# The fifth unit's second matmul: half by seven block products, with the weight sums made earlier

## The chip, the cores and the metric

The kernel runs on one core of a Trainium2 chip. The metric is the device time of one execution in microseconds (us). The kernel before takes 2752.74 us, the median of three runs between 2751.86 and 2753.47. One further execution was recorded by the profiler; every duration below comes from it.

The engines are named as in the profile: PE (matrix products), DVE (vector), ACT (activation and copies), POOL (a second vector engine) and SP, whose queue issues all the data transfers (DMAs) in the order of the program.

## The reference

Two kinds of layer alternate, twice each, on a sequence of 2048 tokens with 1024 channels:

```python
x = A_q
x = x + _A_ref(_layernorm(x), A_k, A_v, A_shift_k, A_ssm_k, A_ssm_D)
x = x + _B_ref(_layernorm(x), B_w1, B_b1, B_w2, B_b2)
x = x + _A_ref(_layernorm(x), A_k, A_v, A_shift_k, A_ssm_k, A_ssm_D)
x = x + _B_ref(_layernorm(x), B_w1, B_b1, B_w2, B_b2)
```

`_A_ref(q, k, v, ...)` takes a causal convolution along the sequence of four taps on `k`, multiplies by `v`, applies a second causal convolution that is as long as the sequence (one filter for each channel), and multiplies by `q`. Only `q` is the layer's input; the convolved signal depends on `k`, `v` and the filters alone, so it is the same in both layers and is computed once. `_B_ref` is the dense part: `h = x @ w1 + b1` (1024 to 3584), `h = relu(h)**2`, `out = h @ w2 + b2` (3584 to 1024). All data is float32.

## The kernel before, in words

**Units.** The sequence is cut into four blocks of 512 tokens. A unit is one layer pair on one block: first the gate with the convolution and two normalisations, then the two dense matmuls. The eight units run in the order `ORDER` (line 25), as (layer, block): (0,0), (1,0), (0,1), (0,2), (1,1), (0,3), (1,2), (1,3). They are numbered from 0, so the fifth unit is unit 4, layer 1 on block 1.

**Precision.** Each float32 operand is split into a rounded high part and the rest, and each product is made of three matmuls: high by high, high by low, low by high (`mm3`, line 326).

**Steps.** The dense part of a unit is a list of steps, written by `add` (line 867). A first-matmul step `m1` uses half of one of the 28 weight tiles of `w1` and makes 12 matmuls of 128x128 by 128x512. A second-matmul step `m2` uses one half-width tile of `w2` and makes 12 as well, three for each of four groups of 128 tokens. A plain unit has four chunks of seven tiles: 56 `m1` and 56 `m2` steps, 112 in all. Within a chunk the first `m2` half is followed by the two `m1` steps of the next chunk's first tile.

**The block products.** In units 5, 6 and 7 (`WINO`, line 51) the second matmul is done in 2x2 blocks with seven products in place of eight (`add_wino`, line 873). Two neighbouring tiles of `h` form a pair, so there are 14 pairs, in four groups of 3, 3, 4 and 4 (`WCH`). A step `w2` handles one product of one pair and makes six matmuls; a pair needs seven of them where plain work needs four `m2` steps of 12. Such a unit has 56 `m1` steps and 98 `w2` steps. Three of the seven products take blocks of `w2` as they are; four take sums of weight blocks. `relu_w` (line 1454) makes the sums of the `h` blocks on DVE (four subtractions or additions and the low parts) and ACT. The results stay in seven accumulators (`wacc`, `load_wacc`, line 1490); `evict_w` adds each finished product to them, by ACT copies the first time where the accumulator is empty; `merge_w` combines them at the end, and `store_w` writes them out. The bias is added to four of them by `add_b2w` on POOL.

**The weight sums.** `make_t` (line 1410) makes the sums of weight blocks once. It works in 28 parts (14 pairs by two column halves): two loads of 256 KB from `w2`, four DVE subtractions of 128x256, two stores of 256 KB into the DRAM tiles `td`. It is a generator: the main loop resumes it once per step, or by a fraction `T_RATE` of a step (lines 1803 to 1809), and it begins when the convolution is done. Its tiles are free buffers of the convolution. A weight load that needs a sum not yet made resumes the generator until it is there (`w_load`, line 973).

**The weight pipeline.** For each step a weight tile is loaded eight steps ahead, its high part is made by ACT (line 997) four ahead and its low part by DVE (line 1005) three ahead. Many split tiles are kept in DRAM after their first use (`wd_m`, `wd_t`); such a pair of 512 KB is read back into one of six `whl` buffers, four steps ahead (line 995), and needs neither ACT nor DVE. In chunk 1 of a unit every tile is such a pair, in other chunks about half.

**What runs beside it.** The long convolution (`prod_stream`, line 511) works through blocks 1 to 3 while the units run. Its products are POOL multiplications (line 517) followed by DVE reductions (line 521); a finished group goes through PE (`inverse`) and is stored in `yd` (line 574). `pace[u]` (line 1666) sets how much of it each step issues: the convolution's whole work for a block divided by the number of steps available less `PACE_SLACK`. `close_conv` (line 1676) issues what is left when the next unit needs it. A block counts as done only in a step's own tick after its last store.

**The next unit's input.** `prep_a` (line 724) reads the next unit's `x` from the 28th step on, in four 512 KB tiles of a ring of two (`px`), and takes statistics. After a plain unit `prep_b` does the gate, the second normalisation and the transposes in the last 18 steps. In units 5 and 6 `prep_w` (line 803) does the first half for each token group early (`W_EARLY`, counted in steps before the end), stores it, and the rest from step 30 before the end on. `load_b2` (line 1638) takes a tile of the same `px` ring for the bias: 12 steps into a plain unit, 34 steps into a unit of block products (line 1693).

**Order.** The engines execute what a step issues in program order. A ring buffer that is asked for again makes the asking instruction wait for the last use of its old content, even if that use is issued in a later step.

Of the kernel before, what the change touches and what calls it, by code (L numbers as in the profile page):

```python
# [46 lines left out]
PACE_SLACK = {1: 74, 3: 10}  # L47
# [187 lines left out]
def tile_h3_mlp(ctx: ExitStack, tc: tile.TileContext, q, kT, vT, shk, ssmT, ssmD, w1, b1, w2, b2,  # L235
# [567 lines left out]
    def prep_w(l, b, lag):  # L803
# [49 lines left out]
        for tt in range(NT):  # L853
            for k, d in enumerate((0, 4, 5, 7)):
                lag.at(W_PREP - W_EARLY[tt] + d, early, tt, k)
            for k, d in enumerate((0, 5, 7, 8, 9)):
                lag.at(W_PREP - W_LATE + 5 * tt + d, late, tt, k)
# [15 lines left out]
    def add_wino(u):  # L873
        p0 = 0
        for c, n in enumerate(WCH):
            pairs = range(p0, p0 + n)
            p0 += n
            for f in range(2 * pairs[0], 2 * pairs[-1] + 2):
                for kh in range(2):
                    add("m1", u, f // FC, f % FC, kh)  # L880
            for j in WORD_END if c == len(WCH) - 1 else WORD:
                for p in pairs:
                    f = 2 * p + (j > 0)
                    wsrc.append(("m2", f // FC, int(j == 2), f % FC) if j < 3 else ("t", p, (j - 4) % 4, 0))
                    if c < len(WCH) - 1:
                        single.add(len(wsrc) - 1)
# [523 lines left out]
    def make_t():  # L1410
        parts = [(p, dq) for p in range(FT // 2) for dq in range(2)]
        got = {}

        def places(n):
            if n < T_FIRST:
                nm, m = (("cp", 3), ("cx", 2), ("cg", 2))[n % 3]
                t = cv.tile([P, 2, 2, 256], F32, name=nm, bufs=m)
                return [t[:, 0], t[:, 1]]
            return [pool.tile([P, 2, 256], F32, name=nm, bufs=m) for pool, nm, m in (
                [(cv, "sm", 2)] * 2, [(const, "fh", 1), (const, "fl", 1)], [(ml, "yt", 2)] * 2)[n % 3]]  # L1420

        def load(n):
            if n < len(parts):
                p, dq = parts[n]
                got[n] = places(n)
# [5 lines left out]
        load(0)  # L1431
        yield
        load(1)
        yield
        yield
        for n, (p, dq) in enumerate(parts):
# [6 lines left out]
            yield  # L1443
            load(n + 2)
            yield
            if n >= T_FIRST:
                yield
# [432 lines left out]
```

## Time and profile before

| | |
|---|---|
| runs | 2752.74 us median (2751.86 to 2753.47) |
| the profiled execution | 2754.0 us, its span 2752.2 us |
| PE busy | 2696.8 us, 98% of the span, 12632 matmuls |
| PE weight loads | 2238.5 us, beside the matmuls |
| DVE busy | 2010.1 us, 73% |
| ACT busy | 1121.7 us, 41% |
| POOL busy | 922.5 us, 34%, nearly all before 1730 us |
| granted PE clock | 0.9955 on average |
| DMA | 755.9 MB, 275 GB/s on average |

The span is the time from the first to the last recorded instruction. A matmul's recorded duration (about 390 ns) overlaps the next one's; the distance between two starts says what one costs. In rows of the timeline the first number is the start, the second the duration. The window rows give the window, its length, the busy time of PE, PE's weight loads, DVE, ACT and POOL with the number of instructions, then the granted PE clock, the busy share of the DMA engines and GB/s. In the rows of waits the numbers are the total wait, the number of waits and the longest, all in us.

### The profile page before, as it was taken

What the parts mean: (1) busy time and instruction counts of PE and PEld (TensorE: products, weight loads), DVE (VectorE), ACT (ScalarE), POOL (GpSimd) and SP (SyncE); (2) the same over time, 40 slices, a digit from 0 to 9 for tenths busy, and PEclk for the clock granted to TensorE, in tenths of its full rate; (3) what the DMA queues carried; (4) which work ended last, traced back from release to release, by engine and by line L of the source; (5) the groups of instructions that cost most, each with busy time, mean ns of one, the idle gap of its engine ahead of it and who ended that gap; (6) DMA issues with size and microseconds to landing.
All of it is one profiled execution on the core that took longest, in us unless ns stands there. A gap on an engine that the chain in (4) does not pass through costs nothing.

```text
span 2752.2 us, 36801 instructions
## 1 busy us (share of the span) xinstructions
PE 2696.8 (98%) x12632; PEld 2238.5 (81%) x12632; DVE 2010.1 (73%) x3109; ACT 1121.7 (41%) x1935; POOL 922.5 (34%) x655
## 2 busy tenths in 40 slices
PE   7899999899999999999999999999999999999999
PEld 6888787788888888888888888888788788878887
DVE  8879888779888877788777665366687666664555
ACT  4254344343444333342234422254455444445443
POOL 6926665155542655326544454000100010001000
PEclk9999999999999999999999999999999999999999
DMA  8489988689989898788987877688888866676546
GB/s 261 164 295 334 306 294 288 238 281 376 345 290 316 306 335 298 257 318 294 344 280 250 314 277 266 226 290 304 297 289 294 281 228 210 230 258 208 176 165 203
DMA packets 378876, 755.86 MB, mean 275 GB/s; under 512 B 43704, under 2 KB 160576, under 8 KB 378688
## 3 DMA queue, kind: packets, MB, share of 16 engines
q1 hardware_dynamic: 378688, 753.50, 79.7%
q8 instruction: 100, 1.64, 0.2%
q14 instruction: 88, 0.72, 0.1%
HBM read 603.41 MB, written 149.95 MB: 274 GB/s over the span
## 4 chain that ended last, share of the span: by engine, by line
PE 84%; DVE 6%; DMA 5%; POOL 2%; issue 1%; ACT 1%; SPq 1%; DVEq 0%; ACTq 0%; POOLq 0%
PE p L327 26%; PE p L329 26%; PE p L328 26%; DMA whl<-wd_m 1%; DMA wr<-w 1%; PE pt L329 1%; PE pt L328 1%; PE pt L327 1%; DVE whl L1005 1%; DMA cg<-gd 1%; DMA whl<-wd_t 1%; PE p L1076 1%; PE pt L446 0%; PE pt L412 0%; PE pt L588 0%
## 5 line engine op out<-in xcount | busy, mean ns | idle before, releaser
L517 POOL TENSOR_TENSOR cp<-cx,cg 128x384 f32<-128x384 f32 (+5 forms) x288 | 540.9, 1891 | 587.7 <-DVE sm L521 383.6
L327 PE MATMUL p<-xh,whl 128*128 128x512 f32 (+1 forms) x1840 | 707.7, 385 | 2.0 <-DMA whl<-wd_m 1.9
L329 PE MATMUL p<-xh,whl 128*128 128x512 f32 (+1 forms) x1840 | 703.8, 382 | 0.6 <-POOL whl L1005 0.6
L328 PE MATMUL p<-xl,whl 128*128 128x512 f32 (+1 forms) x1840 | 703.6, 382 | 0.3 <-DVE xl L1323 0.3
L997 ACT CAST whl<-wr 128x512 fp32r<-128x512 f32 x638 | 384.4, 618 | 458.1 <-PE p L329 269.6
L1005 DVE TENSOR_TENSOR whl<-wr,whl 128x512 fp32r<-128x512 f32 x624 | 506.1, 831 | 72.9 <-ACT whl L997 66.9
L327 PE MATMUL p<-whl,rh 128*128 128x512 f32 x1372 | 547.4, 399 | 6.1 <-DMA whl<-wd_m 4.5
L328 PE MATMUL p<-whl,rh 128*128 128x512 f32 x1372 | 542.4, 395 | 4.2 <-DVE whl L1005 4.2
L329 PE MATMUL p<-whl,rl 128*128 128x512 f32 x1372 | 541.8, 395 | 0.0
L327 PEld LDWEIGHTS p<-xh,whl 128*128 128x128 f32 x1840 | 346.4, 188 | 71.0 <-DMA whl<-wd_m 2.0
L329 PEld LDWEIGHTS p<-xh,whl 128*128 128x128 f32 x1840 | 346.2, 188 | 68.9 <-POOL whl L1005 0.8
L328 PEld LDWEIGHTS p<-xl,whl 128*128 128x128 f32 x1840 | 346.2, 188 | 66.4 <-DVE xl L1323 0.5
L327 PEld LDWEIGHTS p<-whl,rh 128*128 128x128 f32 x1372 | 258.8, 189 | 67.3 <-DMA whl<-wd_m 7.7
L328 PEld LDWEIGHTS p<-whl,rh 128*128 128x128 f32 x1372 | 258.9, 189 | 63.7 <-DVE whl L1005 6.4
L329 PEld LDWEIGHTS p<-whl,rl 128*128 128x128 f32 x1372 | 258.7, 189 | 60.3
L1504 POOL TENSOR_TENSOR acc<-acc,px 128x512 f32<-128x512 f32 x18 | 23.1, 1323 | 774.7 <-DMA px<-b 774.7
L1407 DVE TENSOR_TENSOR rl<-wr,rh 128x512 fp32r<-128x512 f32 x140 | 142.2, 1016 | 179.9 <-ACT rh L1402 179.8
L521 DVE TENSOR_REDUCE sm<-cp 128x128 f32<-128x384 f32 (+5 forms) x288 | 249.0, 873 | 7.9 <-POOL cp L517 7.9
L1399 ACT ACTIVATE wr<-p,b1t 128x512 f32<-128x512 f32 x138 | 95.2, 690 | 371.6 <-PE p L329 369.8
L1468 DVE TENSOR_TENSOR rl<-wr,rh 128x256 fp32r<-128x256 f32 x84 | 49.4, 588 | 206.4 <-ACT rh L1463 206.3
L1527 DVE TENSOR_TENSOR acc<-p,acc 128x512 f32<-128x512 f32 x152 | 101.2, 687 | 89.2 <-PE p L329 88.6
L1460 ACT ACTIVATE wr<-p,b1t 128x512 f32<-128x512 f32 x84 | 57.9, 689 | 187.5 <-PE p L329 187.5
(270 smaller groups left out, 3437.1 us busy)
## 6 DMA issues: line engine op xcount, KB each, us to landing
whl<-wd_m SPq DMA_DIRECT2D x382, 512.0 KB, 5.6
wr<-w SPq DMA_DIRECT2D x494, 256.0 KB, 5.2
wr<-td SPq DMA_DIRECT2D x152, 256.0 KB, 4.4
wd_m<-whl SPq DMA_DIRECT2D x70, 512.0 KB, 6.5
cx<-xd SPq DMA_DIRECT2D x48, 512.0 KB, 5.4
cg<-gd SPq DMA_DIRECT2D x48, 512.0 KB, 6.9
gd<-fg SPq DMA_DIRECT2D x72, 256.0 KB, 6.2
cx<-xd SPq DMA_DIRECT2D x48, 384.0 KB, 6.0
```

The source lines that it names most:

```text
L327: PE.matmul(o, lh, rh, start=start, stop=False)
L328: PE.matmul(o, lh, rl, start=False, stop=False)
L329: PE.matmul(o, ll, rh, start=False, stop=stop)
L517: G.tensor_mul(pr.rearrange("p c i -> p i c"), xt[:, 0:j + 1], gt[:, j::-1])
L521: V.tensor_reduce(sm[:, ty, jj], st["pr"], axis=AX.X, op=OP.add)
L997: A.copy(t[:, 0], raws[n]["t"])
L1005: ENG[e[n % len(e)]].tensor_sub(t[:, 1], raws[n]["t"], t[:, 0].bitcast(F32))
L1399: A.activation(r, st["o"], AF.Relu, bias=b1t[:, st["f"]:st["f"] + 1])
L1407: V.tensor_sub(st["lo"], st["r"]["t"], st["hi"].bitcast(F32))
L1460: A.activation(r, st["o"], AF.Relu, bias=b1t[:, st["f"]:st["f"] + 1])
L1468: V.tensor_sub(st["lo"], r[:, 0:n], st["hi"].bitcast(F32))
L1527: V.tensor_add(accs[tt][:, d], o, accs[tt][:, d])
```

## The change

1. **Unit 4 joins.** `WINO` becomes a table of groups for each unit. Units 5, 6 and 7 keep theirs (written as first pair and count). Unit 4 gets two groups, pairs 7 to 9 and 10 to 13. Its chunks 0 and 1 stay plain (`m1` and `m2` steps), its tiles 14 to 27 go by block products. The unit has 28 `m2` and 49 `w2` steps beside its 56 `m1` steps, 133 in all. The plain chunks' results are added to the accumulators by a new `evict_c`.
2. **The unit's frame.** It thereby takes over what comes with block products: `load_wacc` at step 11 in place of `load_acc` at 5, the bias at steps 34 and 38 in place of 12 and 16, merges and stores of the accumulators into the next unit's first steps, and `prep_w` in place of `prep_b` for unit 5. The early parts of `prep_w` come 76, 69, 45 and 38 steps before the end; units 5 and 6 keep 87, 80, 45, 38.
3. **The weight sums begin with unit 4.** `make_t` takes pairs 7 to 13 first and then 0 to 6. While the convolution is unfinished it works on one part at a time, in the two `yt` buffers, one part in seven steps. Afterwards it works with two loads ahead, in three sets of buffers, one part in five resumptions. It is resumed once per step, in `w2` steps at a rate of 0.85 (unit 4's first group), 0.35 (its second) and 0.7 (later units).
4. **The convolution ends sooner.** `PACE_SLACK` for block 3 goes from 10 to 44 steps. `close_conv` is called 77 steps before the end of unit 4, that is at its step 55.
5. **Kept sums.** Split weight sums are kept in DRAM from unit 5 on, as before; unit 4's are not kept.

The core of the diff:

```diff
-PACE_SLACK = {1: 74, 3: 10}
+PACE_SLACK = {1: 74, 3: 44}
-WINO = (5, 6, 7)
+WINO = {4: ((7, 3), (10, 4)), **{u: ((0, 3), (3, 3), (6, 4), (10, 4)) for u in (5, 6, 7)}}
-W_PREP, W_EARLY, W_LATE = 90, (87, 80, 45, 38), 30
-T_KEPT, T_RATE, T_FIRST, T_AT = 10, 0.6, 10, (0, 3, 1, 2)
-WCH = (3, 3, 4, 4)
+W_EARLY, W_LATE = {4: (76, 69, 45, 38), 5: (87, 80, 45, 38), 6: (87, 80, 45, 38)}, 30
+T_KEPT, T_RATE, T_AT = 10, (0.35, 0.85, 0.7), (0, 3, 1, 2)
...
     def add_wino(u):
+        p0 = WINO[u][0][0]
+        for c in range(2 * p0 // FC):
+            for f in range(FC):
+                if f or c == 0:
+                    for kh in range(2):
+                        add("m1", u, c, f, kh)
+            for dh in range(2):
+                for i in range(FC):
+                    add("m2", u, c, dh, i)
+                if dh == 0:
+                    for kh in range(2):
+                        add("m1", u, c + 1, 0, kh)
+        for c, (first, n) in enumerate(WINO[u]):
+            pairs = range(first, first + n)
+            for f in range(2 * first, 2 * (first + n)):
+                if f == 0 or f > 2 * p0:
+                    for kh in range(2):
+                        add("m1", u, f // FC, f % FC, kh)
...
     def late_kept(key):
...
+        if k == "t":
+            return 5
...
-        if u or not late_kept(wsrc[w]):
+        if u >= late_kept(wsrc[w]):
...
+        n = 0
+        while NB - 1 not in done:
+            load(n, 0)
+            yield
+            yield
+            yield
+            yield from sums(n)
+            yield
+            yield
+            store(n)
+            n += 1
+            yield
+        first = n
+        load(n, 0)
+        yield
+        load(n + 1, 1)
+        yield
+        yield
+        while n < len(parts):
+            yield from sums(n)
+            yield
+            load(n + 2, (n + 2 - first) % 3)
+            yield
+            yield
+            store(n)
+            n += 1
+            yield
...
+    def evict_c(os, wacc, dh):
+        for tt, o in os.items():
+            a = wacc[(1, 2, 3, "x")[2 * (tt // 2) + dh]][tt % 2]
+            V.tensor_add(a, o, a)
...
-            if u in WINO and left == W_PREP:
-                nxt = prep_w(*ORDER[u + 1], lag)
+            if u in WINO and left == W_EARLY[u][0] + 1:
+                close_conv(ORDER[u + 1][1])
+                nxt = prep_w(*ORDER[u + 1], lag, W_EARLY[u])
...
-        if u >= WMAKE and len(done) == NB and not tgen:
+        if u >= WMAKE and not tgen:
             tgen.append(make_t())
         if tgen:
-            town += T_RATE if k == "w2" or u not in WINO and left <= 18 else 1
+            town += 1 if k != "w2" else T_RATE[2 if u > WMAKE else left >= 28]
```

More of the change, by code (lines that the diff above doesn't have):

```diff
@@ L873, in add_wino @@
     def add_wino(u):
[L874 to L881, printed above, removed]
+        p0 = WINO[u][0][0]
[16 more added lines that the diff above has]
+                        add("m1", u, f // FC, f % FC, kh)
+            last = c == len(WINO[u]) - 1
+            for j in WORD_END if last else WORD:
                 for p in pairs:
@@ L1429, in load, with sums @@
                     SY.dma_start(t, src[:, :, dq * 256:(dq + 1) * 256])
[L1431 to L1436, printed above, removed]
+        def sums(n):
             (b00, b01), (b10, b11) = (tuple(t[:, h] for h in range(2)) for t in got[n])
@@ L1442, in make_t, with store @@
             V.tensor_sub(b10, b10, b11)
[L1443 to L1447, printed above, removed]
+        def store(n):
+            p, dq = parts[n]
             for e, t in enumerate(got.pop(n)):
```

32 lines of the change are left out of this document (15 added, 17 removed).

## The prediction

> **What bounds the kernel now.** The page comes first: busy times and the chain that ended last.
>
> ```profile
> span 2752.2 us, 36801 instructions
> PE 2696.8 (98%) x12632; PEld 2238.5 (81%) x12632; DVE 2010.1 (73%) x3109; ACT 1121.7 (41%) x1935; POOL 922.5 (34%) x655
> PE 84%; DVE 6%; DMA 5%; POOL 2%; issue 1%; ACT 1%; SPq 1%; DVEq 0%; ACTq 0%; POOLq 0%
> ```
>
> PE is busy 98% of the span, and the chain lies on it. DVE, at 73%, is next. Next the windows: unit 4 whole, unit 5 whole, parts of unit 5, and one dense stretch of unit 1.
>
> ```profile
> 1543.00:1863.00 320.00, 320.00 (x1436) 263.45 (x1435) 182.88 (x274) 100.96 (x172) 102.65 (x59) 1.00 0.79 277
> 1863.00:2160.00 297.00, 294.06 (x1290) 238.64 (x1290) 223.61 (x429) 145.78 (x241) 10.66 (x8) 1.00 0.87 301
> 1893.20:1922.60 29.40, 29.40 (x128) 23.73 (x127) 21.65 (x40) 17.44 (x30) 0.00 (x0) 1.00 0.78 257
> 1922.60:1960.00 37.40, 35.83 (x156) 28.67 (x155) 22.96 (x49) 15.65 (x26) 10.66 (x8) 1.00 0.89 317
> 2040.00:2100.00 60.00, 60.00 (x263) 48.85 (x262) 48.75 (x96) 24.10 (x41) 0.00 (x0) 1.00 0.89 305
> 2100.00:2160.00 60.00, 58.63 (x269) 47.26 (x268) 48.89 (x85) 33.76 (x57) 0.00 (x0) 1.00 0.85 300
> 619.00:688.00 69.00, 69.00 (x321) 57.38 (x320) 65.27 (x83) 26.80 (x47) 41.52 (x28) 1.00 1.03 375
> ```
>
> PE never idles in unit 4; in unit 5 it idles 2.9 us, 1.6 in 1922.6 to 1960 and 1.4 at the end. In 619 to 688 DVE is 95% busy and the DMA engines are full, yet PE idles nowhere: load on both is not yet a cost. So fewer matmuls in unit 4 shorten the kernel, unless something arrives late. What a matmul costs stands in PE's timeline.
>
> ```profile
> 1542.86 0.39 PE L327 MATMUL p<-xh,whl 128*128 128x512 f32 x1
> 1628.29 0.40 PE L327 MATMUL p<-xh,whl 128*128 128x512 f32 x1
> 1860.55 0.39 PE L327 MATMUL p<-xh,whl 128*128 128x512 f32 x1
> 1893.21 0.40 PE L327 MATMUL p<-whl,rh 128*128 128x512 f32 x1
> 1905.76 0.39 PE L327 MATMUL p<-whl,cx 128*128 128x512 f32 x1
> 1922.56 0.39 PE L327 MATMUL p<-xh,whl 128*128 128x512 f32 x1
> 1942.92 0.50 PE L327 MATMUL p<-xh,whl 128*128 128x512 f32 x1 [1.13 <-DMA whl<-wd_m]
> 2158.26 0.47 PE L327 MATMUL p<-xh,whl 128*128 128x512 f32 x1 [0.31 <-DMA whl<-wd_m]
> 2453.33 0.50 PE L327 MATMUL p<-whl,rh 128*128 128x512 f32 x1 [1.81 <-DMA whl<-wd_m]
> 2455.34 0.77 PE L327 MATMUL p<-xh,whl 128*128 128x512 f32 x1
> 2455.90 0.63 PE L328 MATMUL p<-xl,whl 128*128 128x512 f32 x1
> ```
>
> From 1893.21 to 1905.76 lie 54 block-product matmuls on unsummed blocks of h, 0.2324 us each; from there to 1922.56 lie 72 on summed blocks, 0.2333 each. Unit 4 runs from 1542.86 to 1860.55, 317.7 us; unit 5 to 2158.26, 297.7.
>
> **The change part by part.**
>
> *Fewer matmuls.* 28 `m2` steps of 12 go (336), 49 `w2` steps of 6 come (294): 42 fewer. At 0.2324 us that is 9.8 us, all on PE's path. Of the 294, four products in seven (168) use summed blocks, 0.0009 us dearer: 0.2 back. For a matmul of 512 columns the Trainium skill ("TensorE: Matmul & The Clock Gate", Back-to-back issue gap) gives 512/2.4 + 2.5, about 216 ns, for the isolated spacing; by that the gain would be an estimated 9.1 us. The trace shows 232, and I keep it.
>
> *Weights, evictions, h sums.* By the code's counts, 14 of the 28 old weights came from kept pairs; of the 49 new ones 5 do and 44 are split: 30 more splits on DVE and ACT, 30 more loads of 256 KB and 9 fewer pair reads of 512 KB on SP (0.32 to 0.43 us an issue in the rows below). Per pair of tiles DVE also makes four sums and a long low part, and there are 20 more accumulator additions and merges. None of these is on PE. Their cover is unit 5: its first `w2` stretch has the same 21 split weights and keeps DVE 21.65 of 29.4 us busy with PE never idle. Unit 4's first stretch adds 0.25 resumption of the sums per step, 5 in all or one part (1.7 us below), and loses one of two statistics: about 24 of 29.4, 81%, as in 2040 to 2100, where PE doesn't idle. I take 0.3 us; ends 0 and 3.
>
> *The unit's end.* Merges, stores and the next unit's first loads crowd the queues there. Unit 5 loses 1.4 us so. Unit 6 loses 1.81 before 2453.33, and afterwards PE's starts are 0.56 us apart (2455.34, 2455.90), so a long gap costs more than itself. Unit 4's end has no `wd_t` transfers and is nearest to unit 5's. I take 1.4; ends 0 and 3.5.
>
> *The bias load at step 34.* This is the wait that the change adds.
>
> ```profile
> SPq L715 <- POOL fk L1504: 8.8, 1, 8.8
> 1937.91 0.32 SPq L715 DMA_DIRECT2D px<-x  x1
> 1938.34 0.37 SPq L995 DMA_DIRECT2D whl<-wd_m  x1
> 1643.36 0.33 SPq L715 DMA_DIRECT2D px<-q  x1
> 1649.31 1.27 DVE L686 BATCH_NORM_STATS2 st<-px 128x6 f32<-128x512 f32 x2
> DMA to landing us min/median/max: 3.2/4.2/6.6
> ```
>
> In unit 5 the last `px` load waits 8.8 us until POOL has added the bias that holds its buffer; SP's queue stands, the pair behind it is issued at 1938.34, and PE loses the 1.13 us above (1.6 with its followers). In unit 4 the bias load falls into `prep_a`. Two `px` tiles are in use, so SP stops at step 33 (the pair for step 36 is out by then) until the second statistics, which end at 1643.36 in the trace of before. Step 30 starts at 1628.29 and an `m1` step is 2.72 us, so that is step 35.5. The pair behind it, for step 37, lands a median 4.2 us (the pairs of 1600 to 1740) later, at 37.1: just late. Then the last `px` load waits for the third statistics (1650.6, step 38.2), and the pair for step 40 lands at 39.8. So I take unit 5's 1.6 us; ends 0 and 4 (both pairs at the 6.6 us landing, with followers). POOL's bias additions move from step 16 to 37, still beside the convolution; three product buffers cover them, the convolution's loads that stand behind the bias load on SP are issued two product groups ahead, and chunk 1's weights are pairs that need no DVE.
>
> *The convolution's pace.* Block 3's work is 92.2 in the code's units. Before it goes at 92.2/(2 x 96.8 - 10) = 0.502 a step, after at 92.2/(96.8 + 117.8 - 44) = 0.540 (96.8 and 117.8 are the steps, the last 19 of a unit counted by a fifth).
>
> ```profile
> 1730.76 0.52 SPq L574 DMA_DIRECT2D yd<-wr  x1
> 1725.98 0.75 DVE L554 TENSOR_TENSOR yl<-sm,yh 128x256 fp32r<-128x256 f32 x2
> 1738.29 0.42 DVE L1438 TENSOR_TENSOR cp<-cp 128x256 f32<-128x256 f32 x1
> ```
>
> Its last store is at 1730.76, about step 67.5 of unit 4. The (96.8 + 67.5) x 0.502 = 82.5 done in units 3 and 4 then take 152.7 steps, so it ends at step 55.9, twelve sooner. `close_conv` at step 55 therefore finds it finished: a block counts as done only in a step's tick, which the drain doesn't give. The early store lets the new early loads through. Nothing waits for the convolution, so its end earns nothing; its cover in units 3 and 4 (7.6% more per step) is the dense row 619 to 688. I take 0.
>
> *The sums beside the convolution.* About 8 of 28 parts now run before step 55, when POOL is busy.
>
> ```profile
> L1005 DVE TENSOR_TENSOR whl<-wr,whl 128x512 fp32r<-128x512 f32 x15 | 18.2, 1214 | 6.0 <-ACT whl L997 5.8
> L1005 DVE TENSOR_TENSOR whl<-wr,whl 128x512 fp32r<-128x512 f32 x20 | 13.7, 687 | 10.5 <-ACT whl L997 7.1 <-DMA wr<-w 3.4
> L517 POOL TENSOR_TENSOR cp<-cx,cg 128x1024 f32<-128x1024 f32 x48 | 124.8, 2599 | 138.1 <-DVE sm L521 123.3 <-DMA cx<-xd 14.8
> 1542.90:1730.00 187.10, 187.10 (x842) 154.42 (x841) 110.60 (x122) 51.06 (x89) 102.65 (x59) 1.00 0.77 281
> SPq L1429 <- DMA td<-yt: 5.7, 3, 4.8
> DMA to landing us min/median/max: 5.0/6.1/8.3
> ```
>
> A split takes 1214 ns beside POOL's products (1543 to 1700) and 687 after them (1740 to 1860), 0.53 more. A sum takes 0.42 alone (1738.29), so 0.95 here; a part of four took 1.7 alone. 32 sums are 30 us in the 155 us to step 55 (55 steps of 2.72 or 2.79 and the transforms); the present 110.6 us packed into that time make 141, 91%, below the 95% of unit 1. Each part's load also waits for the last one's store in the one `yt` set: the longest such wait in unit 5 is 4.8 us. A pair is issued about five steps, 13.6 us, before its use; less a 6.1 us landing (619 to 688) 7.5 are left. I take 0. In unit 5 the sums taken away free DVE, but its losses are queue waits: 0, at best 1 us gained. Total sum work and its transfers are unchanged.
>
> Sum: -9.8 + 0.2 + 0.3 + 1.4 + 1.6 = -6.3 us. The profiled execution, 2754.0 us, would be 2747.7; it is 1.3 above the median of the runs, so I forecast 2746.4. The ends give -10.6 and +0.9, or 2742.1 and 2753.6, if all fall together.
>
> **The rivals.**
>
> *A, whole gain.* The waits at step 33 to 40 are absorbed (4.2 us landings leave 37.1 against 37) and unit 5 gains: -9.8 + 0.2 + 0.3 + 0.4, 2743.8. Against it: unit 5 lost 1.6 us by this very wait.
>
> *B, the gain is eaten.* Both queue waits at their upper ends: -9.8 + 0.2 + 0.3 + 3.5 + 4 = -1.8, 2750.9. For it: DMA share 0.83 to 1.0 lengthens landings, and a gap slows PE after it. Against: no unit shows both.
>
> *C, slower: SP starves chunk 1.* Steps 33 to 56 read 24 pairs, one a step; the stops for `px` and for the `yt` set (steps 35, 42, 49) come so close that the queue never regains its five steps, and each pair is 1.13 us late. It decides from 7 late pairs (against 7.9 without the `px` term); with 16 late, 2752.7 - 7.9 + 18.1 = 2762.9. Against it: 7.5 us of slack against stops of 4.8.
>
> *D, slower: DVE blocked by POOL.* If a DVE sum waits out a whole product, 2.6 us, 32 sums cost 32 x 3.0 = 96 us and 110.6 + 96 exceed 155 by 52; a third of it reaching PE through late low parts of h gives 2752.7 - 6.3 + 17 = 2763. The Trainium skill ("SBUF — State Buffer", Who interferes with whom) says just this: a DVE instruction with two SBUF inputs and a POOL instruction that reads SBUF exclude each other for the whole instruction. The 1214 against 687 agrees that they meet, but the mean extra is a fifth of a product.
>
> *E, the block products don't shorten.* If `w2` steps waited on weights, 42 matmuls fewer would be time spent idle: 2752.7. Unit 5's 20 us against unit 4 speak against it.
>
> **How the numbers follow.** Forecast 0.47, A 0.14, B 0.22, C 0.08, D 0.05, E 0.04. A change under 0.2% (5.5 us) can't be told from none. Faster by more than that, under 2747.2: A, and most of the forecast's own range (2744.5 to 2748.3), 0.60. Within: B, E and the forecast's rest, 0.27. Slower: C and D, 0.13. The range, 2742.5 to 2752, leaves out C, D, E and the edge of A.
>
> **What would show it.** Right: 42 matmuls fewer; unit 4 about 311.5 us long; a first sum near 1552; the last `yd` store near 1698; SP standing at the bias load near 1634 to 1643, PE idle by 0.5 to 2 us at steps 37 to 40; unit 4's `w2` spacing 0.233. Wrong: PE waiting for `whl` in steps 42 to 56 (C), DVE over 95% before step 55 with PE waiting for low parts (D), or PE idle within the `w2` groups (E).

## The result and the profile after

The kernel after takes 2763.13 us (median; 2756.91 to 2773.73), the kernel before, on the same chip and beside it, 2757.05 us (2751.86 to 2763.14). The ratio is 1.0023, with a 95% interval of 1.0013 to 1.0032: slower by some 6 us. The forecast was 2746.4, with a range up to 2752.0, so both the number and the sign were wrong.

The page of the kernel after, one execution of 2761.69 us: its span, the busy times, and the chain that ended last.

```profile
span 2759.9 us, 36945 instructions
PE 2691.7 (98%) x12590; PEld 2232.1 (81%) x12590; DVE 2067.3 (75%) x3190; ACT 1143.1 (41%) x1972; POOL 925.9 (34%) x659
PE 78%; DMA 8%; DVE 8%; POOL 3%; issue 2%; SPq 1%; ACT 1%; DVEq 0%; POOLq 0%; ACTq 0%
```

PE has the 42 matmuls fewer, 5 us less busy time, and a smaller share of the chain: 78% in place of 84%, with DMA up from 5 to 8 and DVE from 6 to 8. So PE waits more than it saves.

Where it waits is found from the first matmul of each unit. Units 0 to 2 are the same instructions in both kernels and still differ between executions by up to 9 us (unit 3 starts at 1208.1 in the profile of before, at 1212.8 in that of after, and at 1217.5 in a further one of before, b0 below), so I compare from unit 3 on.

| us | unit 3 | unit 4 | unit 5 | unit 6 | unit 7, to the end |
|---|---|---|---|---|---|
| before | 334.7 | 317.7 | 297.7 | 297.1 | 296.9 |
| before, second profile (b0) | 333.6 | 317.7 | 297.7 | 296.7 | 295.7 |
| after | 336.1 | 324.0 | 297.7 | 295.1 | 294.2 |

Unit 4, which should have become 6.2 us shorter, is 6.3 longer, and most of what follows is about it. Two smaller things go beside it. Unit 3 is 1.4 to 2.5 us longer (the section on e16 comes back to it). Units 6 and 7 together are 3.1 to 4.7 us shorter, with PE idle for 1.9 us in them where it idled 4.0; the prediction had no term for that, and no run isolates its cause.

Unit 4 falls into three stretches: I from its start to step 30, II from there over the rest of chunk 1 and its second matmul to step 58, III to the end of the unit. The windows of before and then of after, in this order (length, then busy PE, weight loads, DVE, ACT, POOL with counts, clock, DMA share, GB/s):

```profile
1542.86:1628.29 85.43, 85.43 (x385) 70.47 (x384) 55.77 (x52) 24.41 (x42) 58.25 (x32) 1.00 0.84 307
1628.29:1706.80 78.51, 78.51 (x349) 64.54 (x348) 41.69 (x54) 18.01 (x32) 38.50 (x22) 1.00 0.82 302
1706.80:1860.55 153.75, 153.75 (x693) 126.54 (x692) 83.17 (x165) 57.91 (x97) 5.89 (x5) 1.00 0.75 246
```

```profile
1548.95:1634.14 85.19, 84.23 (x373) 69.04 (x372) 58.88 (x69) 24.65 (x43) 48.79 (x26) 1.00 0.92 334
1634.14:1723.10 88.96, 82.69 (x362) 66.87 (x360) 50.80 (x71) 18.43 (x33) 42.79 (x30) 0.98 0.87 315
1723.10:1872.96 149.86, 144.27 (x639) 116.45 (x638) 124.75 (x247) 77.58 (x131) 0.00 (x0) 1.00 0.85 291
```

Before, PE is busy in every microsecond. After, it idles 1.0 us in I, 6.3 in II and 5.6 in III. The faster convolution also moves some twelve matmuls of its inverse from I into unit 3 (385 to 373 records in I) and as many from III into II. To count losses alone I use lengths without a stop: I 84.0 (the shortest, in eight of the kernels below), II 80.0 (the kernel e5 below, which is before with the faster convolution), III 152.3 (e5) less the 9.6 us of matmuls that the forecast took off, 142.7. A loss counted so holds both PE's idle time and the slow starts that can follow a stop. By that the kernel after loses 1.2 us in I, 9.0 in II and 7.2 in III, 17.4 in all; the forecast had 3.3 (0.3 + 1.4 + 1.6).

The waits of SP's queue in and around II, first after (1620 to 1715), then before (1600 to 1690); what it waited for, us in total, times, longest, the largest rows of each:

```profile
SPq L1008 <- PE p L328: 19.7, 13, 3.7
SPq L1438 <- DMA td<-yt: 16.8, 4, 4.9
SPq L1674 <- DVE mv L686: 7.9, 1, 7.9
SPq L573 <- ACT whl L1010: 7.2, 1, 7.2
SPq L714 <- DVE mv L686: 2.9, 2, 1.5
```

```profile
SPq L995 <- PE p L329: 59.1, 26, 5.2
SPq L715 <- DVE mv L687: 3.8, 1, 3.8
```

A wait of the pair load (L1008, before L995) for PE is spare lead: SP has nothing to do until PE frees a `whl` buffer. It falls from 59 us to 20. In its place the bias load (L1674) stands 7.9 us at the `px` ring, and the loads of the sums (L1438) stand four times, up to 4.9 us, until the last part's store has left the one `yt` set. (The 7.2 us at L573, a store of the convolution at the end of II, stand in the kernel e3 below as well, 7.3, where II loses nothing.) What that does to the pairs shows in the transfers of the same stretch. After (1640 to 1690): GB/s in 40 slices of 1.25 us, the total, and the pairs with their number, size and median us to landing. Then before (1634 to 1684).

```profile
GB/s 419 419 419 416 413 315 56 13 144 223 315 413 357 383 376 402 424 392 325 270 301 321 406 413 419 419 419 416 403 392 399 407 220 99 339 290 307 288 383 374
DMA packets 6759, 16.89 MB, mean 338 GB/s; under 512 B 594, under 2 KB 3154, under 8 KB 6756
whl<-wd_m SPq DMA_DIRECT2D x14, 512.0 KB, 8.1
```

```profile
DMA packets 4309, 15.45 MB, mean 309 GB/s; under 512 B 480, under 2 KB 480, under 8 KB 4307
whl<-wd_m SPq DMA_DIRECT2D x18, 512.0 KB, 4.4
```

While SP stands at the bias load nothing is issued, and the transfers fall to 56 and 13 GB/s. Later they run at 392 to 419 for ten slices in a row, where the highest slice of the two views is at 424; that this leaves too little rate to win the lead back is likely, but no run tests it by itself. The medians to landing, 8.1 us in place of 4.4, rest on few pairs (the trace tells the landing of 2 of the 14 and of 10 of the 18). The three pairs that PE waited for in II landed 5.2, 7.9 and 6.9 us after their issue. The matmuls of unit 4 that were late (idle time and releaser in brackets) with two that follow the longest:

```profile
1655.17 0.50 PE L326 MATMUL p<-xh,whl 128*128 128x512 f32 x1 [1.37 <-DMA whl<-wd_m]
1659.42 0.47 PE L326 MATMUL p<-xh,whl 128*128 128x512 f32 x1 [1.23 <-DMA whl<-wd_m]
1668.64 0.47 PE L326 MATMUL p<-xh,whl 128*128 128x512 f32 x1 [3.46 <-DMA whl<-wd_m]
1669.40 0.57 PE L326 MATMUL p<-xh,whl 128*128 128x512 f32 x1
1669.77 0.63 PE L327 MATMUL p<-xl,whl 128*128 128x512 f32 x1
...
1757.29 0.51 PE L327 MATMUL p<-whl,rh 128*128 128x512 f32 x1 [1.01 <-DVE whl L1018]
1761.37 0.50 PE L327 MATMUL p<-whl,rh 128*128 128x512 f32 x1 [0.86 <-DVE whl L1018]
1790.12 0.50 PE L326 MATMUL p<-xh,whl 128*128 128x512 f32 x1 [2.27 <-DMA whl<-wd_m]
1870.94 0.50 PE L326 MATMUL p<-whl,rh 128*128 128x512 f32 x1 [1.10 <-DMA whl<-wd_m]
```

In II three pairs are late; after the third the starts are up to 0.43 us apart for a while. In III two low parts from DVE are late in the first block-product group, then a pair at the start of the next first-matmul steps, then pairs at the unit's end.

### The profile page after: what moved, and what is told of

The parts are those of the page before. It is cut to its first block, busy times and chain, and to the rows that moved or that the text cites. A ratio compares the mean times of both kernels' runs of the same rounds, so it can differ in the third digit from the quotient of the medians.

```text
span 2759.9 us, 36945 instructions
## 1 busy us (share of the span) xinstructions
PE 2691.7 (98%) x12590; PEld 2232.1 (81%) x12590; DVE 2067.3 (75%) x3190; ACT 1143.1 (41%) x1972; POOL 925.9 (34%) x659
## 4 chain that ended last, share of the span: by engine, by line
PE 78%; DMA 8%; DVE 8%; POOL 3%; issue 2%; SPq 1%; ACT 1%; DVEq 0%; POOLq 0%; ACTq 0%
PE p L326 24%; PE p L327 24%; PE p L328 24%; DMA wr<-w 2%; DMA whl<-wd_m 2%; DVE whl L1018 1%; PE pt L327 1%; PE pt L326 1%; PE pt L328 1%; DMA td<-yt 1%; DVE sm L520 1%; DMA cg<-gd 1%; DMA whl<-wd_t 1%; DMA cx<-xd 0%; PE p L1089 0%
## 5 line engine op out<-in xcount | busy, mean ns | idle before, releaser
L1010 ACT CAST whl<-wr 128x512 fp32r<-128x512 f32 x668 | 401.8, 619 | 445.5 <-PE p L328 251.3
L1018 DVE TENSOR_TENSOR whl<-wr,whl 128x512 fp32r<-128x512 f32 x654 | 527.8, 829 | 61.6 <-ACT whl L1010 58.8
L326 PE MATMUL p<-whl,rh 128*128 128x512 f32 x1302 | 520.5, 400 | 7.0 <-DMA whl<-wd_m 5.8
L327 PE MATMUL p<-whl,rh 128*128 128x512 f32 x1302 | 516.0, 396 | 7.3 <-DVE whl L1018 7.3
L328 PE MATMUL p<-whl,rl 128*128 128x512 f32 x1302 | 514.8, 395 | 0.0
L1533 POOL TENSOR_TENSOR acc<-acc,px 128x512 f32<-128x512 f32 x24 | 30.6, 1309 | 802.9 <-DMA px<-b 802.9
L326 PEld LDWEIGHTS p<-whl,rh 128*128 128x128 f32 x1302 | 246.1, 189 | 66.1 <-DMA whl<-wd_m 9.7
L327 PEld LDWEIGHTS p<-whl,rh 128*128 128x128 f32 x1302 | 246.3, 189 | 65.3 <-DVE whl L1018 11.1
L328 PEld LDWEIGHTS p<-whl,rl 128*128 128x128 f32 x1302 | 246.0, 189 | 57.2
L520 DVE TENSOR_REDUCE sm<-cp 128x128 f32<-128x384 f32 (+5 forms) x288 | 249.4, 873 | 10.7 <-POOL cp L516 10.7
L1497 DVE TENSOR_TENSOR rl<-wr,rh 128x256 fp32r<-128x256 f32 x98 | 57.5, 587 | 235.2 <-ACT rh L1492 234.8
L1420 DVE TENSOR_TENSOR rl<-wr,rh 128x512 fp32r<-128x512 f32 x126 | 131.4, 1044 | 112.1 <-ACT rh L1415 112.1
L328 PE MATMUL p<-whl,cp 128*128 128x512 f32 x304 | 120.2, 396 | 0.0
```

The costliest lines, as they stand in the source:

```text
L326: PE.matmul(o, lh, rh, start=start, stop=False)
L327: PE.matmul(o, lh, rl, start=False, stop=False)
L328: PE.matmul(o, ll, rh, start=False, stop=stop)
L520: V.tensor_reduce(sm[:, ty, jj], st["pr"], axis=AX.X, op=OP.add)
L1010: A.copy(t[:, 0], raws[n]["t"])
L1018: ENG[e[n % len(e)]].tensor_sub(t[:, 1], raws[n]["t"], t[:, 0].bitcast(F32))
```

## The experiments

Theories: **Q**, the stops of SP's queue use up the lead of the pairs and add up. **M**, the transfers are too many whatever the order of the queue. **V** is rival D, DVE held up by POOL. For stretch III, later, theory **S**: the sums are the cause, by their transfers (**T**) or by their DVE instructions (**D**); theory **A**: ACT standing behind a late statistic. What the expectations call the last third is III. All ratios are to the kernel before on the same chip, with 95% intervals. The losses of the kernels in I, II and III, counted as above:

| | I | II | III | sum | ratio |
|---|---|---|---|---|---|
| after | 1.2 | 9.0 | 7.2 | 17.4 | 1.0023 |
| a0, after again | 1.3 | 9.6 | 6.4 | 17.3 | 1.0024 |
| e1, bias early | 8.6 | 1.0 | 5.9 | 15.5 | 1.0025 |
| e2, two sets | 0 | 7.3 | 6.8 | 14.1 | 1.0009 |
| e3, both | 5.2 | 0 | 7.0 | 12.2 | 1.0002 |
| e6, two sets, bias at 20 | 0 | 1.0 | 8.0 | 9.0 | 0.9999 |
| e8, no sums | 0 | 2.9 | 2.3 | 5.2 | 0.9969 |
| e12, e6 without DVE's sums | 0 | 1.2 | 9.5 | 10.7 | 0.9992 |
| e9, e6 with the root late | 0 | 0.5 | 6.4 | 6.9 | 0.9991 |
| e10, e6 with sums sooner | 1.7 | 4.8 | 5.9 | 12.4 | 1.0002 |
| e11, e9 and e10 | 0 | 6.0 | 5.0 | 11.0 | 0.9993 |
| e14, between e9 and e11 | 0 | 1.7 | 2.0 | 3.7 | 0.9994 |
| e16, e14, bias at 20 everywhere | 0 | 1.9 | 2.2 | 4.1 | 0.9984 |

### The two stops of the queue: a0, e1, e2, e3

*a0* is the kernel after, unchanged.

> The changed kernel itself, so that the next three stand beside it on one chip. All theories: about 6 us above the kernel before (ratio 1.0023).

1.0024 [1.0015, 1.0033], as expected.

*e1* loads and adds unit 4's bias where a plain unit does.

```diff
-                lag.at(34, load_b2, bst)
-                lag.at(38, add_b2w, bst, wacc)
+                lag.at(12 if u == 4 else 34, load_b2, bst)
+                lag.at(16 if u == 4 else 38, add_b2w, bst, wacc)
```

> The changed kernel with unit 4's bias load and additions at steps 12 and 16 instead of 34 and 38, so no px tile is asked for inside the statistics. Theory Q (SP's queue is stopped: by the px ring for 7.9 us and by the single yt set for 32.6 us in eight stops, and together they use up its lead): about 5 us less than the changed kernel (3 to 8), PE's gaps at 1655 to 1673 mostly gone, the yt stops still there. Rival M (the sums' transfers are too much for the DMA engines beside the convolution, whatever the order of the queue): 0 to 2 us less. Rival V (DVE, held up by POOL, is late): 0 to 1 us less.

1.0025 [1.0016, 1.0033]: no gain. The loss in II falls from 9.0 to 1.0 us as theory Q has it, but that in I rises from 1.2 to 8.6. PE's waits in 1560 to 1640, and POOL's additions:

```profile
PE pt L327 <- DVE yl L553: 4.0, 2, 2.5
```

```profile
1591.99 8.05 POOL L1533 TENSOR_TENSOR acc<-acc,px 128x512 f32<-128x512 f32 x6 [4.10 <-DMA px<-b]
```

The eight bias additions hold POOL for 10.8 us, the convolution's next products are late (DVE waits 2.3 us for one), and PE stands in the inverse (`pt`), whose input they make. The cost moved from one queue to another.

*e2* leaves the bias alone and lets the parts made beside the convolution use the `yt` set and the `fy` buffer in turn.

```diff
+            if k == 3:
+                t = cv.tile([P, 2, 2, 256], F32, name="fy", bufs=1)
+                return [t[:, 0], t[:, 1]]
...
-            load(n, 0)
+            load(n, 3 if n % 2 else 0)
```

> The changed kernel with two sets of buffers for the sums while the convolution runs (yt and fy in turn), so that a part's loads no longer wait for the last part's stores. The same bytes, the same DVE work. Theory Q: the 32.6 us of stops on the stores go to under 5, the queue keeps its lead, the px stop alone costs what unit 5 shows (1.6 us): about 8 us less than the changed kernel (5 to 11), near or below the kernel before. Rival M: 0 to 2 us less, since the transfers are the same. Rival V: 0 to 2 us less.

1.0009 [1.0000, 1.0017], 4 us under the kernel after where 8 were expected. The waits of SP's queue in 1620 to 1715:

```profile
SPq L1008 <- PE p L328: 29.5, 15, 5.2
SPq L1677 <- DVE mv L686: 10.8, 1, 10.8
```

The stops for `yt` are gone and the spare lead is partly back, but the stop at the bias load is longer by 3 us, and II still loses 7.3.

SP's timeline says why the stop for `px` costs so much here. The fourth pair behind the bias load, the one for step 40, is issued 12.0 us after it in the kernel after, 8.6 us in e2 and 5.8 us in e8 (below), which makes no sums. Between the two stand the sums' own loads and stores, and in the kernel after a stop of 4.8 us for `yt` as well. PE waits 3.46 us at step 40 in the kernel after, 1.17 in e2 and not at all in e8. The landings differ less: the two pairs that PE waits for in e8 take 5.2 and 7.6 us. The bias load and that pair in after, e2 and e8:

```profile
1649.56 0.33 SPq L1674 DMA_DIRECT2D px<-b  x1
1661.58 0.55 SPq L1008 DMA_DIRECT2D whl<-wd_m  x1
```

```profile
1651.56 0.33 SPq L1677 DMA_DIRECT2D px<-b  x1
1660.15 0.33 SPq L1008 DMA_DIRECT2D whl<-wd_m  x1
```

```profile
1645.23 0.33 SPq L1673 DMA_DIRECT2D px<-b  x1
1651.05 0.44 SPq L1007 DMA_DIRECT2D whl<-wd_m  x1
```

*e3* is both.

> Both edits. Theory Q: 10 to 13 us less than the changed kernel, that is 4 to 7 us below the kernel before, with no PE gap left in unit 4's chunk 1. Rivals M and V: at most 3 us less than the changed kernel, still slower than the kernel before.

1.0002 [0.9994, 1.0011]. II loses nothing: with neither stop there is no late pair, though the sums' transfers are all there. M falls for II, at least for the parts of the sums that the change makes there. The rest is e1's loss in I, and III.

### One part alone: e4, e5

*e4* is the kernel before with the late bias in unit 4 and nothing else.

```diff
-                lag.at(12, load_b2, bst)
-                lag.at(16, add_b2, bst, accs)
+                lag.at(34 if u == 4 else 12, load_b2, bst)
+                lag.at(38 if u == 4 else 16, add_b2, bst, accs)
```

> The kernel before with one thing of the change: unit 4's bias load and additions at steps 34 and 38 instead of 12 and 16. Theory Q (the stops add up: each one uses up part of the lead with which SP issues the weight pairs, and the lead is not won back before the next): the stop for the px buffer is here as long as in the changed kernel, near 8 us, but no stops for the yt buffers go with it, so little reaches PE: 0 to 2 us over before (ratio 1.0000 to 1.0007). Theory P (the stop for px is enough by itself): the gaps of 1655 to 1669 in the changed kernel appear whole, 6 us with their slow matmuls, so +6 us (1.0022).

1.0044 [1.0032, 1.0056], 12 us slower: neither number. SP's waits in 1600 to 1710 and PE's late matmuls:

```profile
SPq L1640 <- DVE mv L687: 11.4, 1, 11.4
SPq L715 <- POOL acc L1644: 10.3, 1, 10.3
...
SPq L715 <- DMA px<-b: 2.5, 1, 2.5
```

```profile
1654.08 0.50 PE L327 MATMUL p<-xh,whl 128*128 128x512 f32 x1 [1.45 <-DMA whl<-wd_m]
1671.55 0.77 PE L327 MATMUL p<-xh,whl 128*128 128x512 f32 x1 [9.01 <-DMA whl<-wd_m]
1672.11 0.63 PE L328 MATMUL p<-xl,whl 128*128 128x512 f32 x1
1672.54 0.63 PE L329 MATMUL p<-xh,whl 128*128 128x512 f32 x1
```

I had counted one stop; the last `px` load then waits for the bias tile to land (2.5 us) and for POOL's additions (10.3) as well, so there are two. The first, 11.4 us, costs PE 1.45; the second, 12.8 us in all and begun two microseconds later, costs 9.01. That is theory Q at its plainest: the first stop is paid from the lead, the next one mostly by PE. II loses 13.3 us.

*e5* is the kernel before with the faster convolution alone (the sums still begin at step 67).

```diff
-PACE_SLACK = {1: 74, 3: 10}
+PACE_SLACK = {1: 74, 3: 23}
...
-        if u >= WMAKE and len(done) == NB and not tgen:
+        if u >= WMAKE and len(done) == NB and (u > WMAKE or last_step[u] - s <= 44) and not tgen:
```

> The kernel before with the faster convolution alone: PACE_SLACK 23 in place of 10, which gives the 0.540 units a step of the changed kernel; the weight sums still begin at step 67 of unit 4 and not before. Theory Q: unit 3 is 1.5 us longer, as in the changed kernel, unit 4 the same as before: 0 to +1.5 us (1.0000 to 1.0006). If the faster convolution were a main part of the loss it would be +3 us or more (1.0011).

1.0012 [1.0004, 1.0021], 3.3 us, above the expected 0 to 1.5: by the times it is the other reading, a main part of the loss. Its profile shows nothing of it: units 3 and 4 together take 651.1 us, in b0 651.3. The section on e16 has what may be the rest.

### The place of the bias, and the sums: e6, e8, b0

*e6* is e2 with unit 4's bias at steps 20 and 24.

> The changed kernel with the sums in two sets of buffers in turn (as e2) and unit 4's bias load and additions at steps 20 and 24: before prep_a asks for the px ring, and later than step 12, where the additions on POOL delayed the inverse. Theory Q: chunk 1 of unit 4 then has no gap and chunk 0 none that e3 put there, 53 us for chunk 1's first-matmul stretch and 60 for chunk 0's; the time falls 8 us below the changed kernel to 2 us under before (ratio near 0.9993). If POOL has no free place and delays the inverse wherever its eight additions stand, it comes out like e3_both, 1.0002.

0.9999 [0.9988, 1.0009], 2 us short of the expectation. I loses nothing and II 1.0, as expected; III still loses 8.0.

*e8* is the kernel after without sums.

```diff
-            while c not in made:
-                next(tgen[0])
-            SY.dma_start(raw, TD[c][:, T_AT[a]])
+            f = 2 * c + a // 2
+            SY.dma_start(raw, w2[f * P:(f + 1) * P, (a % 2) * 512:(a % 2 + 1) * 512])
...
-        if u >= WMAKE and not tgen:
+        if False and not tgen:
```

> The changed kernel without any weight sums: the generator never runs, and the four products that need sums read rows of w2 of the same size in their place, so the output isn't the reference's. Loads and splits of weights stay as they are; 56 loads and 56 stores of 256 KB and 112 sums on DVE go. Theory Q: the stops for the yt buffers go (4 us by e2) and the px stop costs less with the lead intact: 5 to 6 us under the changed kernel, near before (1.0000 to 1.0006). If the losses in the block-product groups (6 us more than forecast) also come from the sums' traffic, they go too: 9 us or more under the changed kernel (0.9990 or less).

0.9969 [0.9957, 0.9980], some 15 us under the kernel after by the two ratios: the second reading. Unit 4 takes 311.9 us, where the forecast had 311.5 with the sums. With the bias stop still there (11.5 us at SP) II loses 2.9, within the forecast's 0 to 4, and III 2.3.

*b0* is the kernel before, profiled beside e9 to e11.

> The kernel before, unchanged, as a run of its own, for a trace taken beside the others. Every theory: ratio 1.0000 within 0.0010. In the traces unit 3 starts at 1208.1 in the kernel before and at 1211.0 to 1216.0 in all kernels made from either, though units 0 to 2 are the same instructions; if that is the chip, unit 3 starts at 1211 to 1216 here too and unit 4 is 317.7 long; if it comes from the edits, it starts near 1208.

1.0001 [0.9993, 1.0010]; unit 3 starts at 1217.5 and unit 4 is 317.70 us long. So the differences in units 0 to 2 do not come from the edits.

### What the sums cost in III: e9, e10, e11, e12, e14

In III of e6, ACT stands 4.4 us at the square root of an early part of `prep_w`, whose statistics DVE has not finished, with the casts of weights queued behind it:

```profile
1743.59 0.29 ACT L693 ACTIVATE sd<-mv,epst 128x1 f32<-128x1 f32 x1 [4.37 <-DVE mv L686]
```

*e9* issues that root one step later.

```diff
                 stats(st["x"], st["mv"][:, 0])
-                st["ve"], st["sd"] = rstd_a(st["mv"])
             elif k == 3:
+                st["ve"], st["sd"] = rstd_a(st["mv"])
+            elif k == 4:
...
-            for k, d in enumerate((0, 4, 5, 7)):
+            for k, d in enumerate((0, 4, 5, 6, 7)):
```

> The kernel e6 (sums in two sets, unit 4's bias at steps 20 and 24) with the square root of prep_w's early parts on ACT issued one step after the statistics that it needs, so that ACT doesn't stand 4.4 us at it in unit 4's first block-product group. Theory A (the two late DVE low parts near 1748 and 1752 follow from ACT standing): these two gaps, 1.9 us, go, and like ones in units 5 and 6 if there are any: 2 us under e6, ratio 0.9992. Theory S (the sums themselves fill DVE and the queues): the gaps stay within 0.5 us, no change against e6 (0.9999).

0.9991 [0.9981, 1.0002]. Of the two late low parts one is gone and the other is 0.61 us; III loses 6.4 in place of 8.0. Theory A holds for 1 to 2 us, little more than the 0.8 by which III differs between the kernel after and its repeat a0.

*e10* makes the sums sooner: five steps a part beside the convolution, rate 0.3 in the first group.

> The kernel e6 with a part of the sums in five steps instead of seven while the convolution runs (11 parts by step 55 instead of 8), and 0.3 resumptions instead of 0.85 per step in the first block-product group. Theory S: the gaps of unit 4's first group and of the first-matmul steps behind it (1.9 and 1.9 us in e6) go, and 0 to 2 us appear in chunks 0 and 1, where DVE and the transfers have more to do: 2 to 3 us under e6, ratio 0.9990. Theory A: the two gaps in the group stay; no change against e6 beyond 1 us.

1.0002 [0.9993, 1.0011]. III gains 2.1 us over e6, II loses 3.8 more: chunk 1 has no room for more parts.

*e11* is e9 and e10 together.

> e9 and e10 together. If both causes count, 4 to 5 us under e6, ratio 0.9983; the kernel without any sums (0.9969) is the bound that neither can pass by much. If only one counts, the same as the better of e9 and e10.

0.9993 [0.9984, 1.0001]: as the better one.

*e12* is e6 with the sums' loads and stores, without the four subtractions.

> The kernel e6 with all loads and stores of the weight sums in their places but without the DVE subtractions, so that the blocks come back unsummed and the output isn't the reference's. From the first-matmul step at 1714 (the start of the last third of unit 4) to the end of unit 4, e6 takes 150.7 us and the kernel without sums and without their transfers 145.0. Theory T (transfers: the 28 MB of the sums fill the DMA engines and SP's queue): 149.5 to 151 here, time as e6 (0.9999). Theory D (DVE: the subtractions make the low parts of the weights late): 145 to 146.5, time near 0.9980. In between, both.

0.9992 [0.9981, 1.0003]. Stretch III of e6, of e8 (no sums), and of e12, with e12's late matmul in its middle:

```profile
1714.42:1865.15 150.73, 144.68 (x639) 116.37 (x638) 125.30 (x248) 77.71 (x131) 0.00 (x0) 1.00 0.86 291
```

```profile
1713.07:1858.03 144.96, 143.85 (x640) 116.67 (x638) 108.98 (x203) 77.50 (x131) 0.00 (x0) 1.00 0.65 217
```

```profile
1719.09:1871.30 152.21, 146.68 (x639) 118.33 (x638) 109.53 (x203) 78.21 (x131) 0.00 (x0) 0.98 0.85 286
```

```profile
1780.72 0.80 PE L326 MATMUL p<-xh,whl 128*128 128x512 f32 x1 [3.92 <-DMA whl<-wd_m]
```

With DVE's 16 us of sums taken out, the two late low parts vanish, yet PE idles 5.5 us as before (6.1 in e6), now mostly for one pair. The transfers, 69 GB/s more than without sums, are enough by themselves: theory T. Without DVE's sums other steps are late, but the loss does not fall (9.5 against 8.0).

*e14* is e9 with six steps a part and rate 0.55.

> The kernel e9 with a part of the sums in six steps instead of seven beside the convolution, and 0.55 resumptions a step instead of 0.85 in the first block-product group: between e9 (chunk 1 of unit 4 in 80.5 us, the last third in 149.1) and e11 (85.9 and 147.7). If the DMA engines are full in chunk 1 (391 GB/s in e6, where the highest slices have 419), each part more costs there what it saves later: ratio as e9, 0.9991 within 0.0005.

0.9994 [0.9984, 1.0004], as expected, but not for the reason given: the loss in III falls to 2.0 and unit 4 to 310.4 us, while unit 5 grows to 300.6, with one gap of 3.17 us. With the rate of the first group at 0.85 III loses 6.4 (e9), at 0.3 and five steps a part 5.0 (e11); why the middle loses least no run shows.

### The bias everywhere: e16, e17

*e16* is e14 with `lag.at(20, load_b2, bst)` and `lag.at(24, add_b2w, bst, wacc)` in all units of block products.

> The kernel e14 with the bias at steps 20 and 24 in units 5, 6 and 7 too, so that no unit of block products has SP stop for the px ring in its chunk 1. Theory Q: unit 5, 300.6 us in e14 with one gap of 3.2 us at 1940, falls to 296 to 297; unit 4 stays near 310 to 312; 3 us under e14, 7 to 8 us under before from unit 3 to the end, ratio 0.9970 to 0.9985. If the gap in unit 5 comes from the sums left over and not from the stop, unit 5 stays near 299 and the ratio near 0.9994.

0.9984 [0.9976, 0.9993]: faster than both kernels, by 4 us than the kernel before. Unit 5 takes 298.1 us (296 to 297 expected). Its unit 4 in the three stretches, and a stop in its unit 3:

```profile
1556.49:1640.52 84.03, 84.03 (x373) 69.10 (x372) 70.57 (x71) 24.85 (x43) 58.19 (x32) 1.00 0.93 347
1640.52:1722.36 81.84, 80.85 (x361) 65.92 (x360) 48.88 (x75) 18.48 (x33) 36.13 (x24) 1.00 0.96 352
1722.36:1867.28 144.92, 143.66 (x640) 116.78 (x638) 121.52 (x241) 77.72 (x131) 0.00 (x0) 1.00 0.86 291
```

```profile
1271.74 0.50 PE L327 MATMUL p<-whl,rh 128*128 128x512 f32 x1 [1.90 <-DVE whl L1019]
...
1273.30 0.63 PE L326 MATMUL p<-whl,rh 128*128 128x512 f32 x1
```

II moves 352 GB/s with 1.0 us idle, where the kernel after moved 315 with 6.3. The stop in unit 3 is a low part late while the faster convolution keeps DVE busy: with its slow followers it makes unit 3 337.9 us long where six of the kernels with the faster convolution take 334.9 to 335.2. The kernel after has one of 1.75 us at the same place, 53 us into the unit, and its repeat a0 has none. Of the fourteen profiles with the faster convolution seven have this stop, of the four without it none. So it belongs to the faster convolution and comes in some executions and not in others; e5's own profile is one without. Whether it makes up the whole of e5's 3.3 us stays open.

*e17* is the kernel before with the bias of units 5 to 7 at 20 and 24 and the root late.

> The kernel before with the two late improvements alone: the bias of units 5 to 7 at steps 20 and 24, the square root of prep_w's early parts one step later. Theory Q: unit 5 loses its 1.6 to 2 us at the bias load, 296 in place of 297.7, units 4, 6 and 7 within 1 us: ratio 0.9993. What e16 gains beyond this is what the change itself is worth once its stops are gone: 5 to 6 us.

1.0004 [0.9996, 1.0013]: no gain. Unit 5 takes 298.9 us: the stop is gone, but POOL's additions now lie in the first block-product group, where DVE's low parts take longer beside them (1905 to 1930: count, busy, mean ns) and one comes late to PE:

```profile
L1006 DVE TENSOR_TENSOR whl<-wr,whl 128x512 fp32r<-128x512 f32 x17 | 17.1, 1044 | 0.2 <-ACT whl L998 0.2
```

```profile
1928.72 0.70 PE L328 MATMUL p<-whl,cx 128*128 128x512 f32 x1 [1.79 <-DVE whl L1006]
```

So what e16 gains is the change's own: unit 4 is 310.8 us in e16 and 317.7 in e17.

## Why the prediction was wrong

**Fewer matmuls, -9.8 + 0.2: right.** 42 are gone. Undisturbed second-matmul starts are 0.2327 us apart in unit 4 of e8 and 0.2324 in before: 630 x 0.2327 - 672 x 0.2324 = -9.6. The trace's 232 ns stands, not the 216 that the Trainium skill gives for the isolated spacing ("TensorE: Matmul & The Clock Gate", Back-to-back issue gap).

**The sums, 0: the step that failed.** The prediction put the sums beside the convolution at 0, for "7.5 us of slack against stops of 4.8", and the rest of them too, for "total sum work and its transfers are unchanged". Without the sums unit 4 takes 311.9 us (e8, forecast 311.5), with them 324.0: they cost 12.1 us, 1.2 in I, 6.1 in II and 4.9 in III.

In II that comparison took one stop by itself. The stop for `px` had just used up the lead: 2.9 us are lost to it without the sums, 7.3 with their loads and stores in the same queue and no stop for `yt` (e2), 9.0 with the stops for `yt` as well. The pair for step 40 goes out 5.8, 8.6 and 12.0 us after the bias load in these three. The 6.1 us landing was not far off. By themselves the stops for `yt` cost 1.0 (e1, II). So the stops do draw on one lead, but most of the price is that of the sums' own loads and stores behind a stop that has emptied it. Whether DVE's part of the sums adds to it in II beside a `px` stop is not shown; without such a stop it adds nothing (e6 and e12).

In III the cover was argued from DVE ("about 24 of 29.4, 81%"). III has 30 weight loads more, and the sums' transfers come on top: it moves 291 GB/s where it moved 246. e12 shows that the transfers are enough to cause the loss without DVE's subtractions. Fullness alone does not settle it: e16 moves 291 GB/s in III too and loses 2.2.

**The bias load, 1.6 (0 to 4): within its ends without the sums.** 2.9 in e8, and the place is as forecast: SP stands from 1641.8 to 1649.6 (forecast 1634 to 1643 for a unit that starts 6.1 earlier), PE idles from step 37 on. What failed is that it was priced as if nothing else were in the queue. In the kernel before the same steps for the bias cost 13.3 us (e4), mostly by a wait for POOL's additions that the prediction did not have; in the kernel after SP has no such wait.

**Weights 0.3 and the unit's end 1.4: right without the sums.** III loses 2.3 in e8 against these 1.7; the 7.2 of the kernel after are the sums'.

**The convolution's pace, 0: open between 0 and 3.** 0 in e5's profile, 3.3 us in its times, a stop of up to 1.9 us in unit 3 in half of the profiles. **Unit 5, 0: right**, 297.7 twice. **Units 6 and 7** had no term and gained 3.1 to 4.7 us.

**The rivals.** C, which was given 0.08 and ruled out by the same comparison, is right in its mechanism and not in its size. The stops for `px` and `yt` do come too close together, but three pairs are late in II and not 16, at steps 37 to 40 and not from 42 on. Its price, 2762.9, meets the measured 2763.1 by luck: it is 10.2 us above 2752.7, where the measured kernel is some 6 us above a kernel before that took 2757.05 beside it; and it has 18.1 us in chunk 1, where II lost 9.0, and 1.7 where III lost 7.2. D falls. For it the Trainium skill ("SBUF — State Buffer", Who interferes with whom) gave the mechanism, a DVE instruction with two SBUF inputs contending with a POOL instruction that reads SBUF. With and without DVE's sums beside POOL, II is 81.0 (e6) and 81.1 us (e12), so none of that cost reaches PE. E falls: the block products save what they should. Rivals A and B took the two queue waits one by one as well.

The range failed for the same reason: its upper end added the ends of single stops and held nothing for the sums.

## What to carry to other kernels

In a queue that issues in order, stops are not priced one by one against the slack: they draw on one lead, and so does every issue that stands behind them. 11.4 us cost 1.45, the next 12.8 cost 9.01 (e4). Add up what stands in the queue until the lead is won back, and read from the timeline when the transfers that matter are issued: 5.8, 8.6 and 12.0 us after the bias load without the sums, with them, and with their stops. When a wait is moved, look for what it meets at the new place: the same bias cost 7 us as a stop of SP (e2), as much as a delay of POOL's products (e1), and 1 at a third step (e6). "Total unchanged" says nothing of a transfer that moves into a stretch where others depend on the same queue.

## What the runs showed of the hardware

**The clock after a gap.** After each of the five stops of PE of more than 3 us (3.17 us in e14, 3.29 in a0, 3.46 in the kernel after, 3.92 in e12, 9.01 in e4) its starts are 0.43 us apart for some microseconds, where they are otherwise 0.23. The granted clock falls with them, to 0.50 from 1669.5 to 1672.9 in the kernel after and from 1666.2 to 1676.4 in e4. After shorter stops it goes either way: 1.90 us in e16, 1.79 in e17 and 1.81 in the kernel before (2453.33) were followed by slow starts, 1.75 and 2.27 us in the kernel after and 1.87 in e3 were not. From unit 3 on no single stop below 1.78 us was, but two of 1.51 and 1.58 us close together were (e3). The Trainium skill ("TensorE: Matmul & The Clock Gate", Part 1) has 426.7 ns for a cold matmul of 512 columns, which the trace meets, and lets the clock fall after an idle window of about 3.4 us; here stops of 1.8 to 1.9 us were sometimes enough.

**A full rate that differs between stretches.** In II of e16 the DMA engines are 96% busy at 352 GB/s, with pairs and the convolution's tiles; in III of e12 85% at 286. By division that is 367 and 336 GB/s at full share. The short rows in which the sums come (3154 of 6759 packets under 2 KB in the view of the kernel after above, 480 of 4309 in before) do not explain it: III of e8, which makes no sums, gives 217 / 0.65, or 334 GB/s. What does is not shown.
